# Sixteen global probability matrices: turned by 32x32 blocks on VectorE and exchanged through HBM, where TensorE transposed them

## The chip, the core and the metric

The kernel runs on one core of one Trainium2 chip. The metric is the device time of one execution in microseconds (us). Three runs of the kernel before the change took 917.84, 916.1 and 916.15 us; their median is 916.15 us. A further execution was recorded by the hardware profiler, and every row of a profile in this text comes from it.

## What is computed

A Longformer-like attention with 8 batches, 8 heads, 512 local positions, 32 global positions and head dimension 64, followed by a two-layer network over all 4352 positions. The part that matters here is the attention of the global queries, which look at every position:

```python
k_all = np.concatenate([k_g, k_l], axis=2)
v_all = np.concatenate([v_g, v_l], axis=2)
s_g = scale * np.matmul(q_g, k_all.transpose(0, 1, 3, 2))
out_g = np.matmul(sm(s_g), v_all)
...
h = x @ w_in
g = np.maximum(h, 0.0) + alpha * np.minimum(h, 0.0)
return (g @ w_out).astype(np.float32)
```

`sm` is a softmax. The matrix `sm(s_g)` has 32 queries by 544 keys for each head. The product with `v_all` sums over the keys, so on TensorE the keys have to stand on the partitions: the probabilities come out with queries on the partitions and must be turned.

## The kernel before

**The work.** The network's part is 144 tiles `t`: nine groups of positions (eight batches of 512 local positions, then one group with all 256 global ones) times sixteen blocks of 128 hidden features. A tile has a first product `f1` (12 matmuls of 128x512 into one PSUM bank named `h_ps`), a bend on ScalarE and VectorE (`leak`, `bend`, tile `g`), a split into a rounded half `gh` (ScalarE) and a rest `gl` (GpSimd), and a second product `f2` (8 matmuls with `gh`, 4 with `gl`) into four banks `o`. `f2` follows its `f1` by two tiles (`LAG = 2`).

**The attention beside it.** The attention runs in pairs of heads `P`, 32 in all, and hides among these tiles. The first eight pairs are in a hand-written order (the long string `ORDER`); from pair 8 on, `plan` puts pair `P` at tile `t = 4(P - 4)`. A local pair has `local_scores` (`s_ps`), a softmax on VectorE and ScalarE (`mn`, `p`), an `exchange` of each half (lines 287 to 293), and `local_values` (`o_ps`) four tiles later. An exchange turns the 16 blocks of 32x32 on VectorE into a staging tile, writes it to HBM in one DMA of 256 KB (`pb`), and reads it back in four DMAs of 64 KB (`pt`), each gathering one block row. The value matmuls wait for those.

**The global part.** Sixteen groups `k`, each with two pairs: one pair is index `e`, the two heads of a pair are index `h`. Group `k` has three planned moments (lines 518 to 526), from `step`, the list 18, 22, 26, 34, 38, 42, ... 90, 98, 106. With `u = step[k]` and `v = step[k+1]`: `load_gn` at `u - 2`; `global_scores` at `u`, which leaves the exponentials in `sg_sb`, a part of the tile `gn`, 128 rows (two halves of the keys, two pairs, 32 queries) by 288 columns for each head `h`; `global_transposes` at `v - 2`; `global_values` at `v`. Most steps are four tiles apart, so `v - 2` is `u + 2`; the third group of each batch has eight tiles to go.

`global_transposes` (lines 391 to 401) issues four TensorE transposes of 128x128 into a PSUM bank `gt`, then one copy on ScalarE and one on VectorE into `sgt_sb`, and four small VectorE transposes of 32x32 for the last 32 keys. `global_values` (lines 403 to 415) multiplies 20 pieces of `sgt_sb` by the values `vg` into a bank named `go`.

**What sets the order.** TensorE keeps the written order throughout (`keep_in_program_order`). From tile 16 on, ScalarE, VectorE and the DMA queue are ordered by the framework's scheduler. All DMAs are issued by SyncE, in one queue (SP in the profile), so a DMA whose input isn't ready holds those behind it. Staging tiles come from one pool of 21 buffers (`stage`, `NST = 21`): whoever takes a buffer waits until its last user is done with it, for a DMA's source until the DMA has landed.

Of the kernel before, what the change touches and what calls it, by code (L numbers as in the profile page):

```python
# [8 lines left out]
F32 = mybir.dt.float32  # L9
# [74 lines left out]
def longformer_ffn(ctx: ExitStack, tc: tile.TileContext, qk, vs, gn, vg, w, alpha, out):  # L84
    nc = tc.nc
    PS = bass.MemoryType.PSUM
    act, vec, dma = Written(tc, nc.scalar), Written(tc, nc.vector), Written(tc, nc.sync)

    const = ctx.enter_context(tc.tile_pool(name="const", bufs=1))
# [3 lines left out]
    dram = ctx.enter_context(tc.tile_pool(name="dram", bufs=1, space=bass.MemoryType.DRAM))  # L93
# [3 lines left out]
    ident = const.tile([128, 128], F32, name="ident")  # L97
    beta_sb = const.tile([128, NF], F32, name="beta_sb")
    pick = const.tile([128, 64], F32, name="pick")
    og_sb = const.tile([128, 128], F32, name="og_sb")  # L100
    sgt_sb = const.tile([128, 5, 2, 64], F32, name="sgt_sb")
    x_raw = const.tile([128, NPAIR, SL], F32, name="x_raw")
    x_glb = const.tile([128, NPAIR, NB * SG], F32, name="x_glb")

# [2 lines left out]
    def matmul(*a, **k):  # L107
        return tc.keep_in_program_order(nc.tensor.matmul(*a, **k))  # L108

    def transpose(*a):  # L110
        return tc.keep_in_program_order(nc.tensor.transpose(*a))  # L111

    def stage(name, dtype=F32):
        return work.tile([128, 512], dtype, tag="st", name=name, bufs=NST)
# [4 lines left out]
    def copy(engine, dst, src):  # L119
        if engine == "a":  # L120
            act.copy(dst, src)
        else:
            vec.tensor_copy(dst, src)

    def bank(tag, name):
        return psum.tile([128, 512], F32, tag=tag, name=name, bufs=2 if tag in "hs" else 1)
# [221 lines left out]
    gns, vgs, sgs, gz = {}, {}, {}, {}  # L348
# [40 lines left out]
        gz[k] = z  # L389

    def global_transposes(k):
        ps, sg_sb = bank("s", "gt"), sgs.pop(k)
        for h in range(2):
            for e in range(2):
                c = 256 * h + 128 * e
                transpose(ps[:, c : c + 128], sg_sb[:, h, 128 * e : 128 * e + 128], ident)
        for h in range(2):
            dst = sgt_sb[:, 0:4, h].rearrange("k (r e) n -> k r e n", r=2)
            copy("ad"[h], dst, ps[:, 256 * h : 256 * h + 256].rearrange("k (e r n) -> k r e n", e=2, r=2))
            for e in range(2):  # L400
                vec.transpose(sgt_sb[0:32, 4, h, 32 * e : 32 * e + 32], sg_sb[32 * e : 32 * e + 32, h, 256:288])

    def global_values(k):
        ps = bank("h", "go")
        for y in range(5):
            for h in range(2):
                for e in range(2):
                    q0 = 64 * h + 32 * e
                    matmul(ps[q0 : q0 + 32, 0:64], sgt_sb[:, y, h, 32 * e : 32 * e + 32], vgs[2 * k + e][:, y, 64 * h : 64 * h + 64], start=(y == 0), stop=(y == 4))
        for e in range(2):  # L410
            del vgs[2 * k + e]
        z = gz.pop(k)
        for h in range(2):
            hs = slice(64 * h, 64 * h + 64)
            act.activation(og_sb[hs, hs], ps[hs, 0:64], AF.Copy, scale=z[hs, 2 + h : 3 + h])
# [79 lines left out]
    def plan(t, where, fn, P):  # L495
        at.setdefault((t, where), []).append((fn, P))
# [13 lines left out]
    for P in range(NRAW, NPR):  # L510
        u = 4 * (P - NPAIR)
# [7 lines left out]
    for k in range(NPR // 2):  # L519
        u, v = step[k], step[k + 1]  # L520
        plan(u - 2, "mid", load_gn, k)
        plan(u, "mid", global_scores, k)
        plan(u + 1, "mid", load_vg, k)
        plan(v - 2, "mid", global_transposes, k)
        at.setdefault((v, "mid"), []).insert(0, (global_values, k))
        plan(v + 1, "mid", global_outputs, k)

# [126 lines left out]
```

## Time and profile before

| | before |
|---|---|
| median of the three runs | 916.15 us |
| the profiled execution's own time | 917.19 us |
| its span, first to last instruction | 915.4 us |
| mean granted TensorE clock | 0.993 |
| TensorE matmul busy | 890.9 us (97%) |
| VectorE busy | 438.6 us (48%) |
| ScalarE busy | 388.1 us (42%) |
| GpSimd busy | 163.1 us (18%) |
| DMA | 140.33 MB, mean 153 GB/s |

In a row of the profile, "L108" is line 108 of the kernel; PE is TensorE's matmul side and PEld its weight load, DVE is VectorE, ACT ScalarE, POOL GpSimd, SPq the queue of SyncE that issues DMAs. `go<-vg,sgt_sb` means "writes `go`, reads `vg` and `sgt_sb`". A timeline row gives start and length in us, then the instruction, how many of it are merged in the row, and in square brackets how long the engine sat idle before it and what ended that. Ends of matmuls are modelled and overlap the next one's start, so the distance from start to start tells what a matmul takes from the engine. A matmul of an fp32 operand that isn't rounded leaves two records.

### The profile page before, as it was taken

What the parts mean: (1) busy time and instruction counts of PE and PEld (TensorE: products, weight loads), DVE (VectorE), ACT (ScalarE), POOL (GpSimd) and SP (SyncE); (2) the same over time, 40 slices, a digit from 0 to 9 for tenths busy, and PEclk for the clock granted to TensorE, in tenths of its full rate; (3) what the DMA queues carried; (4) which work ended last, traced back from release to release, by engine and by line L of the source; (5) the groups of instructions that cost most, each with busy time, mean ns of one, the idle gap of its engine ahead of it and who ended that gap; (6) DMA issues with size and microseconds to landing.
All of it is one profiled execution on the core that took longest, in us unless ns stands there. A gap on an engine that the chain in (4) does not pass through costs nothing.

```text
span 915.4 us, 21219 instructions
## 1 busy us (share of the span) xinstructions
PE 890.9 (97%) x8696; PEld 718.8 (79%) x8704; DVE 438.6 (48%) x840; ACT 388.1 (42%) x1078; POOL 163.1 (18%) x158
## 2 busy tenths in 40 slices
PE   8889998899999999999999999999999999999997
PEld 4568786677887778777887788777887888888897
DVE  6899995354454444554444444554444323111211
ACT  5787873343343344443343344443343333222322
POOL 3000000112111212121112212121122222222221
PEclk9999999899999999999999999999999999999999
DMA  9994335445545454565546454465545330100000
GB/s 330 379 377 169 102 114 164 155 136 188 190 138 192 158 195 146 182 200 186 175 146 195 163 197 146 164 218 183 175 133 171 119 101 24 46 1 1 22 26 24
DMA packets 139953, 140.33 MB, mean 153 GB/s; under 512 B 9296, under 2 KB 112208, under 8 KB 137808
## 3 DMA queue, kind: packets, MB, share of 16 engines
q1 hardware_dynamic: 139856, 138.98, 45.0%
q8 instruction: 68, 1.11, 0.5%
q14 instruction: 29, 0.24, 0.1%
HBM read 111.16 MB, written 27.79 MB: 152 GB/s over the span
## 4 chain that ended last, share of the span: by engine, by line
PE 90%; DVE 4%; DMA 2%; issue 1%; ACT 1%; SPq 1%; DVEq 0%; ACTq 0%
PE o L108 40%; PE h_ps L108 39%; PE o_ps L108 4%; PE s_ps L108 4%; DVE wt L77 2%; PE go L108 1%; PE g_ps L108 1%; SPq L77 1%; DMA ws<-in_w_dram 1%; DMA pb<-pb 1%; PE gt L111 1%; DVE xl L77 0%; PE pt L111 0%; PE gx L108 0%; ACT p L77 0%
## 5 line engine op out<-in xcount | busy, mean ns | idle before, releaser
L108 PE MATMUL h_ps<-xh,wt 128*128 128x512 f32 (+1 forms) x1152 | 339.9, 378 | 0.0
L464 POOL TENSOR_TENSOR gl<-g,gh 128x512 fp32r<-128x512 f32 (+1 forms) x128 | 155.8, 1217 | 744.6 <-ACT gh L77 689.2
L108 PE MATMUL o<-gh,wt 128*128 128x512 f32 (+1 forms) x1152 | 279.1, 385 | 4.1 <-ACT ost L77 4.1
L108 PEld LDWEIGHTS h_ps<-xh,wt 128*128 128x128 f32 x1152 | 212.2, 188 | 41.8 <-issue 0.6
L108 PEld LDWEIGHTS o<-gh,wt 128*128 128x128 f32 x1152 | 205.5, 189 | 48.8 <-issue 6.8
L77 DVE SCALAR_TENSOR_TENSOR g<-g,beta_sb,h_ps 128x512 f32<-128x512 f32 (+1 forms) x144 | 102.2, 710 | 292.9 <-ACT g L77 289.4
L108 PE MATMUL h_ps<-xl,wt 128*128 128x512 f32 (+1 forms) x576 | 217.9, 378 | 0.0
L77 ACT ACTIVATE g<-h_ps 128x512 f32<-128x512 f32 (+1 forms) x144 | 82.0, 570 | 226.2 <-PE h_ps L108 208.6
L108 PE MATMUL o<-gl,wt 128*128 128x512 f32 (+1 forms) x576 | 151.6, 385 | 0.2 <-DVE gl L77 0.2
L77 ACT CAST gh<-g 128x512 fp32r<-128x512 f32 (+1 forms) x144 | 85.7, 597 | 118.7 <-DVE g L77 96.4
L108 PEld LDWEIGHTS h_ps<-xl,wt 128*128 128x128 f32 x576 | 108.4, 188 | 20.3 <-DVE xl L77 0.3
L108 PEld LDWEIGHTS o<-gl,wt 128*128 128x128 f32 x576 | 103.2, 189 | 23.6 <-issue 4.6
L77 ACT ACTIVATE p<-p,mn 128x128 f32<-128x128 f32 x192 | 74.5, 390 | 104.7 <-DVE mn L77 82.4
L77 DVE STREAM_TRANSPOSE pb<-p 128x512 f32<-128x512 f32 x48 | 34.0, 710 | 25.9 <-ACT p L77 25.6
L77 DVE TENSOR_TENSOR xq<-o_ps,rz 128x512 f32<-128x512 f32 x32 | 22.1, 692 | 42.0 <-PE o_ps L108 33.0
L108 PEld LDWEIGHTS o_ps<-vw,pt 128*32 128x32 f32 x2048 | 30.2, 110 | 15.0 <-issue 6.5
L108 PE MATMUL s_ps<-qk 64*32 64x128 f32 x2048 | 38.5, 278 | 3.1 <-issue 3.1
L108 PE MATMUL o_ps<-vw,pt 128*32 128x64 f32 x2048 | 35.8, 221 | 3.0 <-DMA pt<-pb 2.5
L108 PEld LDWEIGHTS s_ps<-qk 64*32 64x32 f32 x2048 | 29.2, 107 | 10.1 <-issue 7.2
L77 ACT ACTIVATION_READ_ACCUMULATOR p<-p,mn 128x1 f32 x192 | 36.0, 188 | 0.0
L77 DVE TENSOR_TENSOR xl<-x_raw,xh 128x512 fp32r<-128x512 f32 x28 | 21.5, 814 | 20.5 <-ACT xh L77 17.3
L77 DVE SCALAR_TENSOR_TENSOR p<-s_ps,mask 128x512 f32<-128x512 f32 x48 | 30.1, 665 | 1.3 <-PE s_ps L108 1.3
(83 smaller groups left out, 547.0 us busy)
## 6 DMA issues: line engine op xcount, KB each, us to landing
vw<-in_vs_dram SPq DMA_DIRECT2D x64, 512.0 KB, 5.3
qk<-in_qk_dram SPq DMA_DIRECT2D x32, 672.0 KB, 6.5
ws<-in_w_dram SPq DMA_DIRECT2D x16, 1024.0 KB, 9.3
pb<-pb SPq DMA_DIRECT2D x48, 256.0 KB, 2.1
pt<-pb SPq DMA_DIRECT2D x192, 64.0 KB, 1.9
vg<-in_vg_dram SPq DMA_DIRECT2D x32, 320.0 KB, 3.4
gn<-in_gn_dram SPq DMA_DIRECT2D x32, 288.0 KB, 4.4
out_dram<-ost SPq DMA_DIRECT2D x32, 256.0 KB, 2.6
```

What stands on the lines that cost most here:

```text
L77: ins = call(*a, **k)
L108: return tc.keep_in_program_order(nc.tensor.matmul(*a, **k))
L111: return tc.keep_in_program_order(nc.tensor.transpose(*a))
L464: (vec if T < NF else nc.gpsimd).tensor_tensor(gl[:, 0:n], gs.pop(T)[:, 0:n], gh_of[T][:, 0:n].bitcast(F32), op=ALU.subtract)
```

## The change

`global_transposes` no longer uses TensorE, PSUM, or ScalarE. Two VectorE transposes per group, one for each `h`, turn the blocks of 32x32 of a 128x256 piece of `sg_sb` into a staging tile `sgb`; one DMA writes that tile to HBM, and four DMAs read it back into `sgt_sb`, in the manner of the local `exchange`. The four small transposes stay. `sgt_sb` keeps its size with another layout, and `global_values` reads its 20 pieces from where they now stand. The planned moment goes from `v - 2` to `u + 1`.

```diff
-    sgt_sb = const.tile([128, 5, 2, 64], F32, name="sgt_sb")
+    sgt_sb = const.tile([128, 640], F32, name="sgt_sb")
+    sgt_main = sgt_sb[:, 0:512]
+    sgt_cut = sgt_main.rearrange("k (r e h c n) -> k r e h c n", r=2, e=2, h=2, c=2)
+    sgt_rest = sgt_sb[:, 512:640].rearrange("k (h n) -> k h n", h=2)
...
     def global_transposes(k):
-        ps, sg_sb = bank("s", "gt"), sgs.pop(k)
+        sg_sb, blk = sgs.pop(k), stage("sgb")
+        for h in range(2):
+            dst = blk.rearrange("k (b h c n) -> k h c b n", b=4, h=2, c=2)[:, h]
+            vec.transpose(dst, sg_sb[:, h, 0:256].rearrange("q (c b n) -> q c b n", c=2, b=4))
         for h in range(2):
             for e in range(2):
-                c = 256 * h + 128 * e
-                transpose(ps[:, c : c + 128], sg_sb[:, h, 128 * e : 128 * e + 128], ident)
-        for h in range(2):
-            dst = sgt_sb[:, 0:4, h].rearrange("k (r e) n -> k r e n", r=2)
-            copy("ad"[h], dst, ps[:, 256 * h : 256 * h + 256].rearrange("k (e r n) -> k r e n", e=2, r=2))
-            for e in range(2):
-                vec.transpose(sgt_sb[0:32, 4, h, 32 * e : 32 * e + 32], sg_sb[32 * e : 32 * e + 32, h, 256:288])
+                vec.transpose(sgt_rest[0:32, h, 32 * e : 32 * e + 32], sg_sb[32 * e : 32 * e + 32, h, 256:288])
+        spread = dram.tile([128, 4, 128], F32, tag="sgb", name="sgb", bufs=2)
+        dma.dma_start(spread, blk.rearrange("k (b n) -> k b n", b=4))
+        for b in range(4):
+            dma.dma_start(sgt_main[32 * b : 32 * b + 32].rearrange("k (w n) -> k w n", w=4), spread[:, b].rearrange("(w k) n -> k w n", w=4))
...
-                    matmul(ps[q0 : q0 + 32, 0:64], sgt_sb[:, y, h, 32 * e : 32 * e + 32], vgs[2 * k + e][:, y, 64 * h : 64 * h + 64], start=(y == 0), stop=(y == 4))
+                    wt = sgt_cut[:, y // 2, e, h, y % 2] if y < 4 else sgt_rest[:, h, 32 * e : 32 * e + 32]
+                    matmul(ps[q0 : q0 + 32, 0:64], wt, vgs[2 * k + e][:, y, 64 * h : 64 * h + 64], start=(y == 0), stop=(y == 4))
...
-        plan(v - 2, "mid", global_transposes, k)
+        plan(u + 1, "mid", global_transposes, k)
```

The built programs show where the instructions stand. On TensorE, at tile 20 before the change, between the first product of the tile (`h_ps`) and the second product of tile 18 (the banks `o`):

```order
L108 MATMUL h_ps<-xh,wt 128x512 x2
L108 MATMUL h_ps<-xl,wt 128x512
L111 MATMUL gt<-ident,gn 128x128 x4
L108 MATMUL o_2171<-gh,wt 128x512 x2
L108 MATMUL o_2172<-gh,wt 128x512 x2
```

The same place of the changed kernel, whose lines from there on stand three further down:

```order
L111 MATMUL h_ps<-xh,wt 128x512 x2
L111 MATMUL h_ps<-xl,wt 128x512
L111 MATMUL o_2171<-gh,wt 128x512 x2
L111 MATMUL o_2172<-gh,wt 128x512 x2
L111 MATMUL o_2173<-gh,wt 128x512 x2
```

The four transposes are gone, and so they are at the fifteen other places; nothing else moves on TensorE.

On VectorE, in the second global group before the change, from the end of its softmax (`gz`) to the next local pair (`xq`, the weighted values; `p`, its scores); a `g` row is the bend of one tile:

```order
L77 RECIPROCAL gz<-gz 64x2
L77 COPY gz<-gz 64x2
L77 SCALAR_TENSOR_TENSOR g<-g,beta_sb,h_ps 128x512 x2
L77 COPY sgt_sb<-gt 128x4x64
L77 TENSOR_TENSOR xq<-o_ps,rz 128x512
L77 STREAM_TRANSPOSE xb<-xq 128x4x4x32
L77 SCALAR_TENSOR_TENSOR p<-s_ps,mask 128x512 x2
```

The same stretch of the changed kernel:

```order
L77 RECIPROCAL gz<-gz 64x2
L77 COPY gz<-gz 64x2
L77 SCALAR_TENSOR_TENSOR g<-g,beta_sb,h_ps 128x512
L77 STREAM_TRANSPOSE sgb<-gn 128x2x4x32 x2
L77 SCALAR_TENSOR_TENSOR g<-g,beta_sb,h_ps 128x512
L77 TENSOR_TENSOR xq<-o_ps,rz 128x512
L77 STREAM_TRANSPOSE xb<-xq 128x4x4x32
```

The copy out of PSUM behind the second bend is gone, and two transposes stand between the two bends.

On the DMA queue of SyncE, between the loads for the next global group (`vg`, `gn`) and the next local pair's values (`vw`), exchange (`xb`, `x_raw`) and queries (`qk`), before:

```order
L77 DMA vg<-in_vg_dram 128x640 x2
L77 DMA gn<-in_gn_dram 128x576 x2
L77 DMA vw<-in_vs_dram 128x8x128 x2
L77 DMA xb<-xb 128x512
L77 DMA qk<-in_qk_dram 128x1344
```

And in the changed kernel:

```order
L77 DMA vg<-in_vg_dram 128x640 x2
L77 DMA gn<-in_gn_dram 128x576 x2
L77 DMA sgb<-sgb 128x512
L77 DMA sgt_sb<-sgb 32x4x128 x4
L77 DMA vw<-in_vs_dram 128x8x128 x2
L77 DMA xb<-xb 128x512
L77 DMA qk<-in_qk_dram 128x1344
```

The write and the four reads stand ahead of `vw`: whatever the queue waits for at them, everything of the next local pair waits behind.

## The prediction

> **What bounds the kernel now.** I read the page's first and fourth parts first: which engine is busy, and what the chain that ended last is made of.
>
> ```profile
> span 915.4 us, 21219 instructions
> PE 890.9 (97%) x8696; PEld 718.8 (79%) x8704; DVE 438.6 (48%) x840; ACT 388.1 (42%) x1078; POOL 163.1 (18%) x158
> PE 90%; DVE 4%; DMA 2%; issue 1%; ACT 1%; SPq 1%; DVEq 0%; ACTq 0%
> ```
>
> The chain is 90% TensorE; VectorE is busy half the time. An average hides stages, so next the busy time by stretch. The sixteen global groups run between 160 and 745 us:
>
> ```profile
> core 0: us, PE busy (x) PEld busy (x) DVE busy (x) ACT busy (x) POOL busy (x), PEclk, DMA share, GB/s
> 145.00:185.00 40.00, 32.09 (x261) 25.19 (x262) 14.27 (x34) 10.95 (x33) 5.09 (x4) 0.91 0.46 146
> 185.00:760.00 575.00, 574.63 (x5997) 461.85 (x5996) 265.76 (x576) 228.45 (x707) 114.44 (x89) 1.00 0.51 168
> ```
>
> In the long stretch TensorE idles 575.00 - 574.63 = 0.37 us in all. Whatever leaves TensorE's queue there shortens the kernel by what it took from the queue, as long as nothing new makes TensorE wait. Whatever is added to VectorE, ScalarE or the DMA queue costs nothing until it becomes such a wait.
>
> **What leaves: four transposes a group.** Their records overlap each other and their neighbours, so I don't use their length but the distance between two matmuls around them. The trace offers the comparison ready-made. Tile 28 has a local pair's `o_ps` behind its second product and no global transposes; tile 32 has the same and the transposes. Timeline of TensorE, tile 28 first:
>
> ```profile
> 237.07 0.39 PE L108 MATMUL h_ps<-xl,wt 128*128 128x512 f32 x1
> 237.30 1.97 PE L108 MATMUL o<-gh,wt 128*128 128x512 f32 x8
> 239.20 1.10 PE L108 MATMUL o_ps<-vw,pt 128*32 128x64 f32 x64
> ...
> 261.17 0.39 PE L108 MATMUL h_ps<-xl,wt 128*128 128x512 f32 x1
> 261.40 0.60 PE L111 MATMUL gt<-ident,gn 128*128 128x128 f32 x4
> 261.76 2.10 PE L108 MATMUL o<-gh,wt 128*128 128x512 f32 x8
> 263.78 1.10 PE L108 MATMUL o_ps<-vw,pt 128*32 128x64 f32 x64
> ```
>
> From the start of the last `h_ps` matmul to the start of `o_ps`: 239.20 - 237.07 = 2.13 us without, 263.78 - 261.17 = 2.61 us with. Four transposes take 0.48 us from the queue. How regular is that, and how many are there?
>
> ```profile
> L111 PE MATMUL gt<-ident,gn x64: 270/272/275, 184.5 to 726.3; 128*128 128x128 f32 x64
> by line: PE o L108 40.3%; PE h_ps L108 38.5%; PE o_ps L108 3.8%; PE s_ps L108 3.6%; DVE wt L77 2.3%; issue 1.2%; PE go L108 1.1%; PE g_ps L108 1.0%; SPq L77 0.9%; DMA ws<-in_w_dram 0.9%; DMA pb<-pb 0.9%; PE gt L111 0.8%; DVE xl L77 0.4%; PE
> ```
>
> 64 transposes are 16 groups, each as long as the others (270 to 275 ns), all between 184.5 and 726.3 us, so all but the first inside the stretch where TensorE never idles (and the first sits 0.5 us ahead of it, between matmuls that follow without a pause). The sum is 16 x 0.48 = **7.7 us**. The chain gives the other bound: 0.8% of 915.4 us is 7.3 us, or 6.9 to 7.8 us by its rounding. I take 7.7, which is measured from start to start.
>
> **What is added, and where it lies.** VectorE: two transposes of 128x256 a group in place of one copy. The trace has no such shape; the rows around it are
>
> ```profile
> L77 DVE STREAM_TRANSPOSE pb<-p 128x512 f32<-128x512 f32 x48 | 34.0, 710 | 25.9 <-ACT p L77 25.6 <-DMA xb<-xb 0.3
> L77 DVE STREAM_TRANSPOSE sgt_sb<-gn 32x32 f32<-32x32 f32 x64 | 12.8, 199 | 22.9 <-ACT gn L77 22.0
> L77 DVE COPY sgt_sb<-gt 128x256 f32<-128x256 f32 x16 | 6.7, 418 | 0.0
> L77 ACT COPY sgt_sb<-gt 128x256 f32<-128x256 f32 x16 | 5.9, 367 | 0.0
> ```
>
> One costs between 0.20 and 0.71 us; on the line through both rows, 256 columns lie at 0.44 us (an estimate). A pair is 0.4 to 1.4 us, I take 0.9; it replaces 0.42 us. The place matters more than the size: the pair now stands between two bends (`g`). VectorE there waits for ScalarE, at the second group and at the worst of all groups:
>
> ```profile
> 211.81 0.75 DVE L77 SCALAR_TENSOR_TENSOR g<-g,beta_sb,h_ps 128x512 f32<-128x512 f32 x1 [4.99 <-ACT g L77]
> ...
> 597.73 0.75 DVE L77 SCALAR_TENSOR_TENSOR g<-g,beta_sb,h_ps 128x512 f32<-128x512 f32 x1 [3.39 <-ACT g L77]
> 599.66 0.75 DVE L77 SCALAR_TENSOR_TENSOR g<-g,beta_sb,h_ps 128x512 f32<-128x512 f32 x1 [1.19 <-ACT g L77]
> ```
>
> 0.9 us fits even into 1.19 us, so the next bend isn't late; at 1.4 us it would be 0.2 us late there, and TensorE needs that bend's results two tiles later. Cost 0. ScalarE loses 0.37 us a group and gains nothing for the end. The transposes read what ScalarE's exponentials left, one tile earlier than before or more; they are long done.
>
> The DMA queue gets five issues a group, and a stop: the reads wait until the write has landed.
>
> ```profile
> pb<-pb SPq DMA_DIRECT2D x48, 256.0 KB, 2.1
> pt<-pb SPq DMA_DIRECT2D x192, 64.0 KB, 1.9
> SPq L77 <- PE o_ps L108: 197.3, 27, 21.8
> ```
>
> The local exchange moves the same sizes: 2.1 us for the write, then four issues of 0.43 us, 1.7 us, and 1.9 us until the last lands. So the queue is held some 3.8 us a group, and the pieces are in `sgt_sb` about 0.9 + 2.1 + 1.7 + 1.5 = 6 us after the bend (1.5, since 0.43 of the last read's 1.9 is its issue). Behind them stands `vw`, and before the change the queue waited for TensorE's `o_ps` at that place, 197.3 us in 27 waits. Is each wait long enough? The second group and, again, the worst:
>
> ```profile
> 207.76 0.86 SPq L77 DMA_DIRECT2D gn<-in_gn_dram  x2
> 214.46 1.01 SPq L77 DMA_DIRECT2D vw<-in_vs_dram  x2
> ...
> 597.10 0.97 SPq L77 DMA_DIRECT2D gn<-in_gn_dram  x2
> 601.90 1.01 SPq L77 DMA_DIRECT2D vw<-in_vs_dram  x2
> ```
>
> In the second group the queue is free from 208.6 to 214.5 us: 5.8 us for 3.8. In the worst the second bend ends at 598.5 us, the transposes at 599.4, the write lands at 601.5, the reads are issued by 603.2, and `vw` is 1.3 us late. Behind it wait `xb`, `qk`, `x_raw`, `pb`, and at the end the `pt` of the next `o_ps`. Those have a reserve; this is among the tightest:
>
> ```profile
> 464.76 1.38 SPq L77 DMA_DIRECT2D pt<-pb  x3
> 470.98 0.71 PE L108 MATMUL o_ps<-vw,pt 128*32 128x64 f32 x36
> ```
>
> The last of these reads is issued at about 465.7 and lands 1.9 us later, 3.4 us ahead of `o_ps`. 1.3 us of delay stays inside. Cost 0. The staging tile `sgb` is a further user of the pool of 21; the next `p` of the local pair takes its buffer in the built program and waits for the write to land: at the worst place that is 601.5 us, and `p` starts here:
>
> ```profile
> 603.27 1.25 DVE L77 SCALAR_TENSOR_TENSOR p<-s_ps,mask 128x512 f32<-128x512 f32 x2
> 224.73 0.77 PE L108 MATMUL go<-vg,sgt_sb 128*32 128x64 f32 x40
> ```
>
> The last row is who needs the pieces: `go` of the second group, at 224.7 us, against 206.8 + 6, or 214 us by way of the queue (free at 208.6, then 2.1 + 1.7 + 1.5). Ten us of reserve.
>
> By the Trainium skill's page "VectorE: DVE Perf Modes", section "Rules for kernel authors", a 128x128 transpose belongs on TensorE where PSUM will do, because VectorE turns blocks of 32x32 alone; the exchange is the price of that. The rule would be right here if the exchange were waited for. By the Trainium skill's page "DMA: Bandwidth & Descriptors", section "Anatomy of one DMA — SWDGE (gpsimd) path", a DMA issued from GpSimd takes 2.0 us plus its bytes over 436 GB/s; taken over to these, issued from SyncE, an estimate for the write and one read is 2.6 + 2.2 = 4.8 us, 77 us for sixteen on the path. The rows above have 2.1 + 1.9 = 4.0 us, and the reserve of `go` says that none of it is on the path.
>
> **The sum.** 917.19 us (the profiled execution) - 7.7 = 909.5 us. That execution is 1.0 us above the median of the three runs; by the median, 916.15 - 7.7 = 908.45, and since it is the median that is compared, I predict **908.5 us**. With the chain's 6.9 us and 0.5 us for the spread of the runs the forecast spans 907.5 to 910.
>
> **The rivals.**
>
> *Part is given back at the group boundaries.* When a batch ends, output copies, splits and exchanges fight for the staging pool, and one more user shifts who gets which buffer. For: in four of the sixteen groups `sgb` takes over a buffer of an output tile, free only when its DMA has landed, which takes up to 4.7 us:
>
> ```profile
> DMA to landing us min/median/max: 1.7/2.5/4.7
> ```
>
> Against: 0.37 us of idle in the long stretch shows how much slack there is. Four boundaries of up to 1.2 us each, about 5 us: 911 to 914 us.
>
> *A stall longer than the clock's patience.* The one such stall in the trace, at tile 18, where output copies came late:
>
> ```profile
> 171.09 3.78 PE L108 MATMUL o<-gh,wt 128*128 128x512 f32 x8 [4.10 <-ACT ost L77]
> 174.67 1.81 PE L108 MATMUL o<-gl,wt 128*128 128x512 f32 x4
> ```
>
> TensorE waits 4.10 us, and then eight matmuls take 174.67 - 171.09 = 3.58 us, 0.45 each instead of 0.23 (the granted clock of that stretch is 0.91 in the windows above); for the twelve of that product 2.6 us more, 6.7 us in all. If VectorE, held at the new transposes for a buffer, lets bend and output copies be late at two boundaries, 2 x 6.7 - 7.7 makes it **slower**, 922 us. It decides once TensorE waits there for over 7.7 us in all. Against: the second bend of the four groups is ready about when the outputs land, and TensorE uses it two tiles later. By the Trainium skill's page "TensorE: Matmul & The Clock Gate", section "Why this matters for your kernels", a gap of over about 3 us halves the clock; the row agrees, 0.45 us a matmul against 0.23.
>
> *Nothing is gained.* TensorE is shown busy, but is held by something the profile doesn't show, and the 0.48 us return as a wait: 916 us. Against: 2.13 and 2.61 us, to a hundredth.
>
> *The stall at tile 18 goes.* It lies ahead of the first new instruction, so only chance would do it: 902 us.
>
> **Chances.** Forecast 0.80, part given back 0.08, slower 0.05, nothing gained 0.04, stall gone 0.03. A difference of 0.2%, 1.8 us, is about what a measurement of this kernel can tell from none. Faster: 0.80 + 0.08 + 0.03 = 0.91; within: 0.04; slower: 0.05. The range is the forecast's span, widened on both sides into the neighbours: 906 to 912 us.
>
> **What would show it.** TensorE: no `gt`, the distance from `h_ps` to `o_ps` 2.13 us at every pair, idle in the long stretch still under 1 us, 7.7 us less span. VectorE: pairs of 0.9 us between bends, `g` no later. Queue: `sgb` landing in about 2.1 us, `vw` late at one or two places by at most 1.5 us, `go` never waiting for a DMA. Wrong it would be if TensorE waits for a bend, a `pt` or `go`, above all at batch ends.

## The result: 926 us, about 1% slower, and where the profile shows it

| | before, run beside it | after |
|---|---|---|
| median | 917.0 us | 926.2 us |
| the profiled execution | 917.19 us | 927.19 us |
| ratio after / before, 95% interval | | 1.0105 (1.0069 to 1.0141) |
| predicted | | 908.5 us (906 to 912) |

By the prediction's bound of 0.2% the change makes the kernel slower. 7.7 us were to be saved; about 9.6 us (1.05% of 917) were lost, so something that the forecast put at nothing costs some 17 us.

The changed kernel's page, its parts on busy time and on the chain that ended last, and the long stretch by windows:

```profile
span 925.4 us, 21216 instructions
PE 892.3 (96%) x8640; PEld 716.2 (77%) x8640; DVE 440.5 (48%) x856; ACT 383.4 (41%) x1062; POOL 163.0 (18%) x158
PE 71%; DMA 15%; SPq 6%; DVE 4%; ACT 2%; issue 2%; DVEq 0%; ACTq 0%
185.00:760.00 575.00, 564.31 (x5826) 449.99 (x5825) 263.77 (x586) 221.82 (x687) 112.97 (x88) 0.99 0.56 181
```

TensorE, idle for 0.37 us in that stretch before, now idles 10.69 us there. The chain says who holds it: DMA went from 2% to 15% and SyncE's queue from 1% to 6%.

First what came as forecast. On TensorE's timeline of the changed kernel, the place at tile 32 from which the transposes left, and VectorE's new pair among the costliest groups:

```profile
260.22 0.39 PE L111 MATMUL h_ps<-xl,wt 128*128 128x512 f32 x1
260.45 1.97 PE L111 MATMUL o<-gh,wt 128*128 128x512 f32 x8
262.35 1.10 PE L111 MATMUL o_ps<-vw,pt 128*32 128x64 f32 x64
L77 DVE STREAM_TRANSPOSE sgb<-gn 128x256 f32<-128x256 f32 x32 | 12.2, 421 | 1.7 <-DMA out_dram<-ost 1.7
```

262.35 - 260.22 = 2.13 us, where it was 2.61; a pair takes 0.84 us on VectorE. Now the queue: what SyncE waited for (total, times, longest), and the issues of `sgb` with their size and median time to landing:

```profile
SPq L77 <- PE o_ps L111: 88.1, 12, 21.8
SPq L77 <- DMA sgb<-sgb: 68.1, 16, 6.1
sgb<-sgb SPq DMA_DIRECT2D x16, 256.0 KB, 4.9
```

The write lands after 4.9 us (median), and the queue stands still for 68.1 / 16 = 4.3 us a group; from the issue of `sgb` to the end of the last read's issue it is held 6.9 us (mean of the sixteen in the trace). Its waits for `o_ps`, which were its slack, fell from 197.3 us in 27 waits to 88.1 in 12: at 15 places it now comes too late to wait. One such place, ahead of the batch that starts at 360 us. The queue's timeline before:

```profile
336.59 0.85 SPq L77 DMA_DIRECT2D gn<-in_gn_dram  x2
344.30 1.01 SPq L77 DMA_DIRECT2D vw<-in_vs_dram  x2
345.77 0.64 SPq L77 DMA_DIRECT2D xb<-xb  x1
352.43 1.75 SPq L77 DMA_DIRECT2D x_raw<-xb  x4
354.28 0.38 SPq L77 DMA_DIRECT2D pb<-pb  x1
358.50 0.34 SPq L77 DMA_DIRECT2D pb<-pb  x1
```

and after:

```profile
337.10 0.87 SPq L77 DMA_DIRECT2D gn<-in_gn_dram  x2
338.06 0.38 SPq L77 DMA_DIRECT2D sgb<-sgb  x1
344.45 2.53 SPq L77 DMA_DIRECT2D sgt_sb<-sgb  x4
347.08 1.02 SPq L77 DMA_DIRECT2D vw<-in_vs_dram  x2
...
353.52 1.75 SPq L77 DMA_DIRECT2D x_raw<-xb  x4
355.37 0.38 SPq L77 DMA_DIRECT2D pb<-pb  x1
...
359.25 0.38 SPq L77 DMA_DIRECT2D pb<-pb  x1
```

From the issue of `sgb` to `vw` nine microseconds pass. `vw` is 2.8 us later than before, although TensorE by then is 3 us ahead of its former time. Who waits at the end? ScalarE's casts of the next batch's `x`, and TensorE's first product with them; before:

```profile
360.79 1.66 ACT L77 CAST xh<-x_raw 128x512 fp32r<-128x512 f32 x3 [3.59 <-DMA pb<-pb]
362.61 0.62 PE L108 MATMUL h_ps<-xh,wt 128*128 128x512 f32 x2
363.06 0.39 PE L108 MATMUL h_ps<-xl,wt 128*128 128x512 f32 x1
363.29 0.62 PE L108 MATMUL h_ps<-xh,wt 128*128 128x512 f32 x2
```

and after (ScalarE's row first in both):

```profile
361.37 1.66 ACT L77 CAST xh<-x_raw 128x512 fp32r<-128x512 f32 x3 [3.32 <-DMA pb<-pb]
360.01 0.39 PE L111 MATMUL h_ps<-xl,wt 128*128 128x512 f32 x1
362.04 0.73 PE L111 MATMUL h_ps<-xh,wt 128*128 128x512 f32 x2 [1.64 <-ACT xh L77]
```

`xh` is split off into staging buffers. In the built programs of both kernels the first `xh` of these batches takes the buffer of one `pb` and the second that of the next `pb`, so each waits until that write has landed; the other two take buffers of other tiles and follow on ScalarE. Before, the second cast was done at about 361.4 us (three in 1.66 us from 360.79) and needed at 363.29: 1.9 us of reserve. At the five starts of batches in the trace this reserve is 1.5 to 3.1 us.

In the changed kernel the second cast begins 0.6 us later than before (361.37), while TensorE, without the transposes, is at the batch 3 us sooner (359.56 against 362.61): together more than the reserve. TensorE's lead alone isn't the cause. In the kernel without the round trip (the first experiment) the casts come sooner with it, and the reserve at the five starts is 1.5 to 4.1 us. The hold keeps the casts from following.

The stall then costs more than its length. Windows around the three longest, after (PE busy, and the granted clock, are the columns to read), and the same windows before:

```profile
358.00:368.00 10.00, 8.31 (x28) 5.84 (x26) 4.00 (x6) 4.04 (x8) 1.61 (x2) 0.83 0.25 79
464.00:478.00 14.00, 10.45 (x73) 7.36 (x75) 3.99 (x6) 4.60 (x8) 2.23 (x2) 0.76 0.18 58
574.00:584.00 10.00, 7.53 (x39) 5.18 (x42) 3.81 (x6) 4.00 (x7) 1.31 (x2) 0.83 0.25 79
```

```profile
358.00:368.00 10.00, 10.00 (x66) 8.03 (x68) 4.29 (x7) 4.26 (x8) 1.74 (x3) 1.00 0.24 72
464.00:478.00 14.00, 14.00 (x182) 11.36 (x182) 8.21 (x15) 6.77 (x21) 2.56 (x2) 1.00 0.43 138
574.00:584.00 10.00, 10.00 (x163) 8.13 (x162) 6.31 (x13) 4.20 (x20) 1.27 (x1) 1.00 0.59 201
```

Counted from start to start over 185 to 760 us of the changed kernel: eight distances between successive matmuls are over 0.6 us, together 11.8 us longer than a matmul's 0.23 (six of them, 9.9 us, are waits for `xh` at the starts of batches); 26 are of 0.43 us, 5.2 us more; seven others over 0.4 us make 1.8 us. That is 18.8 us, where the kernel before has 0.5.

### The profile page after: what moved, and what is told of

Its sections match the earlier page's. It is cut to its first block, busy times and chain, and to the rows that moved or that the text cites. A ratio compares the mean times of both kernels' runs of the same rounds, so it can differ in the third digit from the quotient of the medians.

```text
span 925.4 us, 21216 instructions
## 1 busy us (share of the span) xinstructions
PE 892.3 (96%) x8640; PEld 716.2 (77%) x8640; DVE 440.5 (48%) x856; ACT 383.4 (41%) x1062; POOL 163.0 (18%) x158
## 4 chain that ended last, share of the span: by engine, by line
PE 71%; DMA 15%; SPq 6%; DVE 4%; ACT 2%; issue 2%; DVEq 0%; ACTq 0%
PE o L111 32%; PE h_ps L111 31%; SPq L77 6%; DMA xb<-xb 4%; DMA pb<-pb 4%; DMA sgb<-sgb 3%; PE s_ps L111 3%; DMA qk<-in_qk_dram 3%; PE o_ps L111 2%; PE go L111 1%; ACT p L77 1%; DMA ws<-in_w_dram 1%; PE g_ps L111 1%; DVE wt L77 1%; DVE gm L77 1%
## 5 line engine op out<-in xcount | busy, mean ns | idle before, releaser
L111 PE MATMUL h_ps<-xh,wt 128*128 128x512 f32 (+1 forms) x1152 | 344.3, 382 | 8.8 <-ACT xh L77 8.8
L111 PEld LDWEIGHTS o<-gh,wt 128*128 128x128 f32 x1152 | 208.4, 191 | 50.8 <-issue 6.3
L77 DVE TENSOR_TENSOR xl<-x_raw,xh 128x512 fp32r<-128x512 f32 x28 | 18.7, 714 | 44.0 <-ACT xh L77 44.0
```

The costliest lines, as they stand in the source:

```text
L77: ins = call(*a, **k)
```

## The experiments

All ratios are to the kernel before, run on the same chip, with 95% intervals.

| run | median, us | ratio |
|---|---|---|
| the changed kernel | 926.2 | 1.0105 (1.0069 to 1.0141) |
| no round trip | 912.4 | 0.9928 (0.9903 to 0.9954) |
| `sgb` out of the pool | 937.7 | 1.0188 (1.0140 to 1.0236) |
| exchange on GpSimd | 977.5 | 1.0635 (1.0592 to 1.0679) |
| before, step moved early | 917.3 | 0.9989 (0.9959 to 1.0018) |
| reads that don't wait | 915.3 | 0.9963 (0.9939 to 0.9987) |
| no reads | 913.3 | 0.9926 (0.9902 to 0.9949) |
| step at `u + 2` | 914.0 | 0.9939 (0.9912 to 0.9965) |
| loads behind the exchange | 914.6 | 0.9935 (0.9906 to 0.9964) |
| step at `v - 2` | 917.9 | 0.9974 (0.9954 to 0.9994) |
| both mends | 930.2 | 1.0109 (1.0085 to 1.0132) |
| before plus exchange, into `sgt_sb` | 956.9 | 1.0389 (1.0360 to 1.0417) |
| before plus exchange, into a dead corner | 925.7 | 1.0068 (1.0038 to 1.0098) |
| third groups at `u + 2` | 913.8 | 0.9953 (0.9931 to 0.9975) |
| the other eleven at `u + 2` | 917.5 | 0.9982 (0.9959 to 1.0006) |

**No round trip.** What is the change worth if nothing is exchanged?

```diff
-        sg_sb, blk = sgs.pop(k), stage("sgb")
+        sg_sb, blk = sgs.pop(k), sgt_main
...
-        dma.dma_start(spread, blk.rearrange("k (b n) -> k b n", b=4))
...
```

> The changed kernel with VectorE's two transposes writing straight into sgt_main; the write to HBM and the four reads are left out, so the global probabilities that go uses are not exchanged and the output differs. Four theories. Q (the SyncE queue is held while the sgb write lands): 16 stops go, the time falls to about 909 us, TensorE idles under 1 us between 185 and 760 us. S (sgb as one more user of the staging pool): sgb is not taken, about 909 us. B (the 16 x 512 KB of extra transfers slow the other transfers): none are left, about 909 us. V (VectorE's pair, or the step standing one tile after the scores, makes a bend or a p late): nothing of that is changed, about 926 us.

0.72% faster, 6.6 us of the 7.7 predicted; TensorE idles 2.8 us in the long stretch, not under 1. VectorE's work, its place and TensorE's saving are all in this kernel, so V falls, and the loss of 1.0105 - 0.9928 = 1.77%, 16.2 us, is that of the buffer, the write and the reads. The count of start-to-start distances has 3.6 us over 0.23 in this run and no slow matmul: 18.8 - 3.6 = 15.2 of the 16.2 us.

**`sgb` out of the pool.**

```diff
-        sg_sb, blk = sgs.pop(k), stage("sgb")
+        sg_sb, blk = sgs.pop(k), big[0][:, 0:512]
```

> The changed kernel with the transposed block in the part of the large tile that held the group's keys (free once the scores are through), not in the staging pool of 21; the write, the four reads and their queue are as in the changed kernel, only one of the two next loads of keys is issued behind them. S: the pool is as before the change, about 909 us, and xh no longer waits at the starts of the batches. Q and B and V: about 926 us, stalls of 2 to 3 us at the starts of the batches stay.

Not faster but 1.9% slower than before, and `xh` waits as in the changed kernel. Waits by engine, this run first, then the changed kernel:

```profile
ACT xh L77 <- DMA pb<-pb: 38.2, 10, 6.5
PE h_ps L111 <- ACT xh L77: 11.2, 5, 2.9
```

```profile
ACT xh L77 <- DMA pb<-pb: 36.4, 10, 5.9
...
PE h_ps L111 <- ACT xh L77: 8.8, 6, 2.7
```

A user less in the pool doesn't help, so S falls as the main cause. The run isn't clean, since one load of keys stands behind the reads in it; why it is slower than the changed kernel wasn't followed. The run without reads, below, keeps the buffer and says the same.

**Exchange on GpSimd.**

```diff
-        dma.dma_start(spread, blk.rearrange("k (b n) -> k b n", b=4))
+        nc.gpsimd.dma_start(spread, blk.rearrange("k (b n) -> k b n", b=4))
```

(and so for the reads.)

> The changed kernel with the sgb write and its four reads issued from GpSimd, so that SyncE's queue never stops for them; bytes, buffers and VectorE's work unchanged. Q: about 909 us, the waits of SyncE's queue on sgb (68 us) are gone and its waits on o_ps are back near 190 us. S, B and V: about 926 us.

6.4% slower, which no theory had. The waits by engine show why this run can't decide:

```profile
POOL sgt_sb L405 <- issue: 152.0, 45, 5.8
ACT g L77 <- POOL gl L469: 92.4, 15, 8.7
PE go L111 <- DVE g L77: 42.1, 10, 6.6
```

SyncE's waits on `o_ps` are back (250.3 us), and TensorE waits for no `xh`. But GpSimd computes `gl`, and the exchange now holds that engine: ScalarE waits 92.4 us for `gl`, VectorE's bend for ScalarE, and TensorE at `go` for the bend. What holds GpSimd is mostly not the write's landing (11.4 us in three waits); it is 152.0 us of idle time between its issues, for which the profile shows no releaser. With a loss of its own this large, the run decides nothing.

**Before, step moved early.**

```diff
-        plan(v - 2, "mid", global_transposes, k)
+        plan(u + 1, "mid", global_transposes, k)
```

> The kernel before, its four TensorE transposes and their copies moved to one tile after the scores, as the change moves its step. V, where it is the place in the program that costs: some us over 917. Q, S and B: 917 us within 2.

No difference that can be told. The place by itself costs TensorE's version nothing that shows.

**Reads that don't wait; no reads.** Bytes against waiting. In the first, the write stays and each read takes 64 KB of the key input:

```diff
-            dma.dma_start(sgt_main[32 * b : 32 * b + 32].rearrange("k (w n) -> k w n", w=4), spread[:, b].rearrange("(w k) n -> k w n", w=4))
+            dma.dma_start(sgt_main[32 * b : 32 * b + 32].rearrange("k (w n) -> k w n", w=4), gn[0, :, 128 * b : 128 * b + 128].rearrange("(w k) n -> k w n", w=4))
```

> The changed kernel with its sgb write kept and its four reads of the same size and shape taken from the key input, which is there from the start, so that no read waits for the write; the output differs. Q (the queue stops while the write lands): no wait on sgb is left in SyncE's queue, 909 to 912 us. B (the 16 x 512 KB of transfers themselves): bytes are all there, about 926 us.

In the second the reads are gone.

> The changed kernel with the sgb write kept and the four reads left out, so the global probabilities are not exchanged and the output differs. Q: nobody in the queue waits for the write, 909 to 912 us. B: half of the bytes are left, about 918 us. W (the write's landing holds its staging buffer, which a p or an xh takes next): about 926 us.

0.9963 and 0.9926. With every byte moved but nobody waiting for the write, 1.0105 - 0.9963 = 1.4% of the 1.8% come back, and `xh` takes the same buffers as in the changed kernel. B falls as the main cause. For the bytes and the issues some 0.35% remain, 3 us (0.9963 - 0.9928); it is more than expected, and the two intervals overlap. Without the reads the time is that of no round trip, so the write's buffer (W) costs nothing that shows either.

**Step at `u + 2`; loads behind the exchange.** Both keep the computation whole and change the stop, in two ways. One tile later, the scheduler puts the reads behind `vw` and `xb`:

```diff
-        plan(u + 1, "mid", global_transposes, k)
+        plan(u + 2, "mid", global_transposes, k)
```

> The changed kernel with its step planned one tile later (two tiles after the scores). In SyncE's queue the write then stands behind the four loads and ahead of vw as before, but vw and the write of xb stand between it and its reads. Q: the write has landed when the reads' turn comes, the queue waits for sgb under 10 us in all and only the issues (27 us in sixteen groups) remain, 909 to 915 us, and faster than before. B: about 926 us.

In the other, `load_vg`, `load_gn` and the exchange are kept in program order, the exchange first:

```diff
-        plan(u + 1, "mid", load_vg, k)
         plan(u + 1, "mid", global_transposes, k)
+        plan(u + 1, "mid", load_vg, k)
...
+            dma.on = True
             dma.dma_start(vgs[P], vg[P])
+            dma.on = False
```

(and so around the loads of `gn` and the exchange's five DMAs.)

> The changed kernel with the sgb write and its reads issued ahead of the group's loads of vg and gn rather than behind them. If the write lands late because those loads are ahead of it (4.3 us waited instead of the 2.1 us of pb), the queue's wait on sgb falls from 68 to about 34 us; by Q some of the loss goes, 912 to 920 us; if the loads don't matter for the landing, 68 us and 926 us stay. B: about 926 us.

0.9939 and 0.9935, both faster than before and nearly where no round trip is. The queue's waits of the first; then those of the second, and the issue row of its `sgb`:

```profile
SPq L77 <- DVE sgb L77: 74.7, 16, 12.8
SPq L77 <- DMA sgb<-sgb: 0.3, 2, 0.2
```

```profile
SPq L77 <- DMA sgb<-sgb: 30.1, 16, 4.0
sgb<-sgb SPq DMA_DIRECT2D x16, 256.0 KB, 2.1
```

The same write of the same size lands in 2.1 us with the loads behind it and in 4.9 us right behind them. In the first run the queue no longer waits for the landing: the reads follow behind the wait for `xb` that it has anyway. Instead it waits 74.7 us for VectorE's transposes, ahead of `vw`, while its waits for `o_ps` fall from the 197.3 us of before to 95.3. So this stop isn't gone but stands in the queue's slack. In neither profile does TensorE wait for `xh`; in the second it waits for the rest `xl` at two starts of batches, 2.6 us in all. In both, a staging buffer changed hands as well; what that is worth is taken up under "Which groups?".

**Step at `v - 2`; both mends.**

> The changed kernel with its step where it stood before the change (two tiles before the group's values); for eleven of sixteen groups that is the same tile as in the run one tile later. Q: write and reads stand apart in the queue as there, 910 to 915 us, faster than before. If the place is indifferent: 926 us.

0.9974: 915 us by the ratio, faster than before by little. It seems less than at `u + 2`, though the intervals overlap and only the third groups and the last one differ (ten stand at the same tile, not eleven). In it VectorE's output copies wait for `pb`, 21.0 us in 5 waits against 14.3 at `u + 2`, and three distances at TensorE's second products are 1.2 to 1.7 us. The step there may meet the output copies of the batch's end; this wasn't followed further. The buffers of `xh` are those of the changed kernel here, and TensorE never waits for `xh`.

> The changed kernel with both mends: its step two tiles after the scores, so that the reads stand behind vw and the write of xb, and the write ahead of the loads of vg and gn, which come behind the reads. Q: no wait on sgb is left and xb's write is not behind these loads either, 909 to 913 us, at or a little under either mend alone. If the loads, now next to qk, make x_raw or go late: 915 us or more.

1.0109: the second theory held. The loads now stand between `xb` and `qk`, and they come late themselves (waits of TensorE):

```profile
PE g_ps L111 <- DMA gn<-in_gn_dram: 3.7, 5, 1.2
PE go L111 <- DMA vg<-in_vg_dram: 2.1, 5, 0.7
PE s_ps L111 <- DMA qk<-in_qk_dram: 1.8, 1, 1.8
PE h_ps L111 <- ACT xh L77: 2.2, 3, 1.2
```

These four make 9.8 of the some 16 us by which it is slower than either mend; the rest wasn't followed. Two mends that each work don't add here: what is moved out of one transfer's way stands in another's.

**Before plus the exchange.** Does the hold cost by itself, with TensorE's transposes kept?

```diff
+    def global_exchange(k):
+        sg_sb, blk = sgs[k], stage("sgb")
...
+        plan(u + 1, "mid", global_exchange, k)
         plan(v - 2, "mid", global_transposes, k)
```

> The kernel before, with the four TensorE transposes and their copies kept, and the exchange added beside them at the change's place (VectorE's two transposes, the write, four reads into sgt_sb, which the copies overwrite later). If the exchange's loss stands apart from what TensorE saves (Q): the time lost is that between the changed kernel and the one without the round trip, 926 - 909 = 17 us, so about 933 us, and not under 925, with stalls at the starts of the batches. If the loss came from TensorE's shorter groups and not from the exchange: 917 us.

3.9% slower, 36 us, far more than either theory has, and for another reason, seen in ScalarE's waits and TensorE's:

```profile
ACT sgt_sb L77 <- DMA sgt_sb<-sgb: 24.0, 7, 5.8
PE s_ps L108 <- DVE sgt_sb L77: 22.4, 6, 5.6
```

The copies out of PSUM wait for the reads, keep the bank, and `s_ps` waits for the bank. The run is inconclusive; it was repeated with the reads into a part of the tile `gn` that nobody reads:

> The kernel before with the exchange added as in the run before, but its reads go into a dead corner of the large tile that nobody reads (for lack of room half as wide, 32 KB each, their number and their wait as before), so that no copy waits for them. If the hold of the queue costs by itself, with nothing taken from TensorE: 925 to 933 us, with TensorE waiting for xh at the starts of the batches. If the added exchange fits beside TensorE's four transposes and only the shorter groups expose it: 917 to 920 us.

0.68% slower, 6.2 us (3.5 to 9.0): 923 us by the ratio, between the two theories. Its waits have

```profile
PE h_ps L108 <- ACT xh L77: 2.7, 3, 1.5
```

so TensorE waits for `xh` three times and 2.7 us in all, against six times and 8.8 us in the changed kernel. So the hold costs without the change's saving, but 6 of the 16 us only. The other 10 appear together with the shorter groups (argued, not shown: the half-width reads may have a part in it).

**Which groups?** The third group of each batch alone, and the other eleven alone:

```diff
-        plan(u + 1, "mid", global_transposes, k)
+        plan(u + 2 if k % 3 == 2 else u + 1, "mid", global_transposes, k)
```

> The changed kernel, with the step of the third group of each batch alone (5 of 16, the last before the batch's end) two tiles after the scores instead of one; the other eleven as in the changed kernel. If the hold costs where little reserve is, in the chain from vw to xb, x_raw and pb that the next batch's xh waits for: nearly all comes back, 911 to 916 us. If each hold costs alike: 5/16 of the 12 us between the changed kernel and the one with all sixteen moved come back, about 922 us.

> The mirror of it: eleven groups two tiles after the scores, the third of each batch one tile after them, as in the changed kernel. If the loss sits at the batches' ends: 921 to 926 us. If each hold costs alike: 5/16 of 12 us over 914, about 918 us.

0.9953 and 0.9982. With five groups moved, 1.0105 - 0.9953 = 1.52 of the 1.66% that all sixteen bring (1.0105 - 0.9939) come back. But these five alone cost only 0.9982 - 0.9939 = 0.43%, not the 1% or more that the mirror run's first theory had, and about what equal shares give; and the intervals of these two overlap. The holds don't add up.

These two runs alone can't place the loss, for they differ in one thing more. In the built programs of the step at `u + 2`, the loads behind the exchange and the third groups at `u + 2`, the second `xh` of a batch takes the buffer of a `gh`, not that of the second `pb`, and no longer waits for that write. In the changed kernel, the other eleven, the step at `v - 2` and the three runs without a wait on the write it takes that of the `pb` (in "both mends" the third `xh` does). How much would the old buffer have cost? An estimate from the landing of the second `pb` in each trace and 0.7 us for the cast behind it: at `u + 2` the cast would still have been done 0.3 to 3.3 us ahead of its product at all five starts, so the new place of the stop is enough there. With the loads behind it would have been late at four starts, by 0.1 to 2.1 us, and with the third groups moved at two, by 0.8 and 1.3 us. So in these two a part of the gain may be the buffer's; no run separates it.

The run with the other eleven is free of this, since its buffers are those of the changed kernel. Its third groups still stop the queue (24.8 us in five waits), yet TensorE waits for `xh` at two starts of batches only, 2.2 us in two waits, against all five in the changed kernel, 8.8 us in six. So the lateness of earlier groups does carry over to the batch's end: at four of the five starts the wait is shorter or gone without it. At the fifth, the place at 360 us, it is 1.64 us in both runs.

The queue's timeline of the run with five groups moved, at the place shown above:

```profile
337.89 0.86 SPq L77 DMA_DIRECT2D gn<-in_gn_dram  x2
340.11 0.33 SPq L77 DMA_DIRECT2D sgb<-sgb  x1
340.83 1.37 SPq L77 DMA_DIRECT2D vw<-in_vs_dram  x2
...
350.68 0.38 SPq L77 DMA_DIRECT2D pb<-pb  x1
```

`vw` is issued 6.2 us sooner than in the changed kernel (340.83 against 347.08), `pb` 4.7 us sooner. TensorE doesn't wait for `xh` in this run, only for `xl`, 1.1 us in two waits.

## Why the prediction was wrong, point by point

- **"The sum is 16 x 0.48 = 7.7 us."** Right, within the measurement: without the exchange 6.6 us are gained (4.2 to 8.9 by the interval), and the distance is 2.13 us in the changed kernel too.
- **VectorE, "cost 0".** Right. The estimate of 0.44 us a transpose was 0.42, and the run without the round trip has the pair at the same place.
- **"2.1 us for the write ... So the queue is held some 3.8 us a group."** This step failed first: the term was mis-sized. The write lands after 4.9 us, and the queue is held 6.9 us a group. The size was taken from `pb`, a write that follows nothing heavy in the queue. `sgb` stands right behind two loads of `vg` and two of `gn`, 320 and 288 KB each; the run with the loads behind it (2.1 us) shows that they make the difference. A row nearer in this respect was in the table of DMA issues: `xb`, the same 256 KB behind `vw`, 5.5 us.
- **"`vw` is 1.3 us late", at the worst place only.** It is 2.8 us late at the place shown, and at 15 of the places where it waited for `o_ps` the wait is gone. The lost waits alone aren't the loss: with the loads behind the exchange there are 12 left as well, and the time is 0.9935. The working took each group by itself, with the full idle ahead of it; the run with the other eleven moved shows that lateness carries over.
- **"Those have a reserve ... 1.3 us of delay stays inside. Cost 0."** The second failure, and the one that turned the sign: the wait put at nothing costs 16.2 us (the changed kernel against no round trip). The reserve looked at was that of `pt` at an `o_ps` in mid-batch, 3.4 us. At a batch's start the same queue has another customer, `xh`, with 1.5 to 3.1 us by the trace of before, and it isn't in the list. With the predicted 3.8 us the queue would still have been in time at the place shown, where it stood idle for 6.9 us before (337.44 to 344.30); with the 9.0 us that pass in fact it isn't. So listing `xh` alone would not have shown the stall at this place; it takes the longer hold as well.
- **The staging pool** ("the next `p` ... takes its buffer"). It did wait, 7.6 us in six waits on VectorE, with little effect: with the buffer taken but no reads the loss is gone. One of the waits, 2.43 us at 425 us, stands ahead of a late bend, for which TensorE waits 0.50 us at `go`.
- **`go`, ten us of reserve.** Right as far as DMAs go: only in "both mends", where `vg` is moved, does the profile put a wait of TensorE at `go` down to one.
- **The rival "a stall longer than the clock's patience", 922 us.** The nearest, with a chance of 0.05: the place (batch ends), the slow clock after the stall and the sign were right. Its cause was not. It held VectorE for it, waiting for output copies; it was the queue, by way of `xh`. And it counted two stalls of one size, where there were eight of different sizes, six of them at `xh` and three with slow matmuls behind.

## What to carry to other kernels

A DMA that waits inside an in-order queue has two prices: its own landing, which depends on what was issued just ahead of it, and everything queued behind it; so take its duration from a row with the same neighbours, and list every consumer of what stands behind, at the places where the program changes phase too, before calling the wait hidden. Where such an exchange is wanted, put the reads behind another wait that the queue has anyway: here the same exchange one tile later made a loss of 1% a gain of 0.6%. Slack in a queue is a stock for all groups together, not an allowance for each. And a step that moves can change which tile takes whose buffer: compare the buffers of two versions before a gain is put down to the place.

## What the runs showed of the hardware

The same write of 256 KB landed in 4.9 us (median of 16) where four loads of some 300 KB were issued just ahead of it in the same queue, and in 2.1 us where they came behind it. Where the queue first waited for VectorE between these loads and the write (the step at `u + 2`), it was 2.2 us.

TensorE's clock fell after a shorter idle than the tile-18 stall had suggested: 1.64 us of idle at 360 us (2.03 us from start to start) were followed, from 363.6 us on, by eight matmuls of 0.43 us, and the granted clock was 0.83 over 358 to 368 us. In the run with the other eleven groups at `u + 2`, a gap of the same 2.03 us and 1.64 us of idle left the granted clock at 1.00 (360 to 372 us), and so did one of 1.88 us in the last run with the exchange added (466 to 478 us). The length of the gap alone doesn't say how much is lost.
